# Attention, MLP and expert routing on one core: two chunks keep their low parts in SBUF across a branch, and the branch's verdict is loaded earlier

## The chip, the cores and the metric

The kernel runs on one core of a Trainium2 chip. Engines are written PE (matmuls; PEld is its loading of the stationary operand), DVE, ACT, POOL and SP (which here only issues DMAs). The metric is the device time of one execution in microseconds, median of several runs; lower is better.

## The reference, cut to what matters

```python
x = attention_with_random_features(q, k, v, omega)   # (2304, 512)
h = x @ w_in                                         # 512 -> 2048
m = (h - np.tanh(h)) @ w_out                         # 2048 -> 512
logits = m @ w_gate                                  # 8 experts
# the largest logits are served first; an expert takes at most 288 tokens
for e in range(8):
    out[assigned == e] = np.maximum(m[assigned == e] @ w1[e], 0) @ w2[e]
```

The MLP in the middle is where the change lies.

## The kernel before

**Numbers.** A value in float32 is held as a high part (type fp32r) and a low part (what is left). A product is made of three matmuls: high by high, high by low and low by high. In the code a name with H is a high part, with L a low one.

**Tiling of the MLP.** The 2304 tokens are 6 blocks of 384; the hidden 2048 are 16 chunks `f` of 128. `chunk_ops` makes a chunk of the hidden layer (12 matmuls at L601 to L603 into a PSUM bank, then `h - tanh h` by a polynomial of the range |h| < 0.18: ACT L605 and L625, DVE L626 and L628). `hidden_ops` splits the result into `gH` (ACT, L298) and `gL` (DVE or POOL, L303). `m2_ops` multiplies a chunk by its rows of `w_out`: for each of the block's three token tiles `t` three matmuls at L648 (nine for a chunk), added up over `f` in the PSUM tile `acc[t]`. `wo` is the high part of `w_out` and stays in SBUF; its low parts lie in DRAM (`lows`), and `split_ops` loads that of a chunk into `oL`, a ring of three buffers (SP, L563).

**Blocks 4 and 5.** Their hidden layers are made side by side, chunk by chunk (`mlp_ops`, from "j, lacc4, lprev4" on). The logits of both are summed meanwhile from the hidden layer (`last_logits`, matmuls at L719 and L721, and after the last chunk a copy `lt` on ACT, transposes at L732 and copies to `lg` on DVE at L736 and L737). Block 5 keeps all of `gH5` and `gL5` in SBUF. Block 4 ("the last but one") keeps its 16 high parts in the place of `wi`, which is used up; its low parts go to DRAM (`g4l`, SP L800) through `gLr`, a ring of four buffers, and come back from there (SP L822) when `but_last_ops` multiplies block 4 by `w_out`. Of this, chunks 0 to 2 (`NHERE`) are multiplied before the branch.

**The branch.** `range_ops` works out one number, `over` (DVE, last instruction L868), that says whether some |h| may leave the polynomial's range or some weight is too small. After block 5's logits every engine loads `over` into a register (`values_load`, L1458) and branches on it (L1459). For these inputs the body of the branch, which makes the MLP again in a general way, is skipped.

**Behind the branch**, in order of need: the chunks 3 to 15 of block 4 (117 matmuls), the copies of `acc` to `xm` (`out_ops`), the 16 chunks of block 5 (`last_ops`, 144 matmuls, L648 too), the experts (L1333 to L1354). Beside it runs the routing. `best_ops` finds each token's best expert on DVE (L989 to L993). `search_ops` finds the logit at which the first expert is full, in seven digits: comparisons on DVE (`r_cmp`, L1030), counts on PE (nine matmuls at L1036), the digit on DVE (L1055, L1057) and its spreading by a matmul on PE (L1061), then the next digit. After the digits follow some 10 us of placing, the loads of that expert's weights (`r_wraw`, SP L1249) and the next search.

**What sets the order.** `Plan` is a list scheduler that runs while the program is built. Each operation has engines, a cost, a due time (`plan.at` plus `lag`) and buffers from rings; `Plan.run` gives out the operation that can start first by these costs, and among those of one time the one that is due first. That fixes the order on every engine; on the chip each engine goes through its list and waits by semaphores. `Plan.run` is called once for all before the branch, and once for all behind it, where all engines start at the same planned time. A ring's buffer comes free after the last operation that the plan knows to use it.

Of the kernel before, what the change touches and what calls it, by code (L numbers as in the profile page):

```python
# [185 lines left out]
def tile_kernel(ctx, tc, q, k, v, omega, w_in, w_out, w_gate, w_gate_t, w1, w2, out, dbg=None):  # L186
# [79 lines left out]
    def sring(where, shape, dtype, name, n):  # L266
        return plan.ring(shape, dtype, name, [(where, [f"{name}{i}" for i in range(n)], False)])
# [21 lines left out]
    sr = sring(wmid, [P, BLK], F32, "s", 5)  # L289
    gHr = sring(wmid, [P, BLK], F32R, "gH", 2)  # L290
    gLr = sring(wkeep, [P, BLK], F32R, "gL", 4)
    xmr = sring(wout, [P, DM], F32, "xm", 3)
    g5r = [plan.ring([P, BLK], F32R, n, []) for n in ("gH5", "gL5")]
    mTr = sring(wmid, [P, NC, P], F32, "mT", 1)

    def copy(e, out, in_):
# [7 lines left out]

    bT = Buf(None)

    def omega_ops():
        for i in range(2):  # L310
# [277 lines left out]
    def chunk_ops(j, f, x, wsp, general, gH=None, gL=None):  # L588
# [18 lines left out]
        if general:  # L607

            bg, df = Buf(gen[1]), Buf(gen[1])
            big = lambda: bg.t.bitcast(I32)  # L610
            dif = lambda: df.t
            plan.op(DVE, 0.5, lambda e: V.tensor_scalar(big(), ut(), TMAX ** 2, None, op0=OP.is_gt), r=[u], w=[bg], lag=2.6)
            plan.op(DVE, 0.5, lambda e: V.tensor_scalar(ut(), ut(), TMAX ** 2, None, op0=OP.min), r=[u, bg], w=[u], lag=2.6)
            plan.op(ACT, 0.5, lambda e: nc.scalar.activation(dif(), ph(), AF.Tanh), r=[p], w=[df], lag=2.6)
# [25 lines left out]
    def m2_ops(f, g, wsp, acc, prev, fine=False):  # L640
        gH, gL = g
        oH, oL = wsp
        out = list(prev or [None] * TPB)
        for t in range(TPB):
            def m2(e, i, t=t):
                c = slice(t * P, (t + 1) * P)
                for k in i:
                    nc.tensor.matmul(acc[t].t, (gL if k == 2 else gH).t[:, c], (oL if k == 1 else oH).t,  # L648
                                     start=(f == 0 and k == 0), stop=(f == NF - 1 and k == 2), skip_group_check=True)

            for i in ([0], [1], [2]) if fine else ([0, 1, 2],):
                out[t] = plan.op(PE, 0.235 * len(i), lambda e, i=i, m2=m2: m2(e, i), r=[gH, gL, oH, oL], w=[acc[t]],
                                 after=[out[t]] if out[t] else [], lag=0.65 * t)
        return out

    def out_ops(j, t, acc):
        n = j * TPB + t
        xm = Buf(xmr)
        plan.op({ACT: 0.48, DVE: 0.6}, 0, lambda e: copy(e, xm.t, acc.t), r=[acc], w=[xm])
        return xm, plan.op(SP, 0.47, lambda e: nc.sync.dma_start(ms[n * P + 1:(n + 1) * P + 1, :], xm.t), r=[xm], lag=0.7,  # L660
                           nbytes=P * DM * 4)

    def gate_ops(j, t, xm):
        n = j * TPB + t
        tp, mT, lp = Buf(bank), Buf(mTr), Buf(bank)
        lgb = Buf(None)

        def transposes(e):
            for c in range(NC):
                nc.tensor.transpose(tp.t[:, c * P:(c + 1) * P], xm.t[:, c * P:(c + 1) * P], ident)  # L670
# [73 lines left out]
    def mlp_ops(start, step, general=False):  # L744
# [41 lines left out]
        for f in range(NF):  # L786
            plan.at = start[j] + step[j] * f - LEADI
            wsp = split_ops("wi", f)
            if not general:
# [3 lines left out]
            plan.at += step[j] / 2  # L793
            chunk_ops(j + 1, f, x[j + 1], wsp, general, *g5[f])
            plan.at = start[j] + step[j] * f
            gH, gL = Buf(None, wi[:, f, :BLK]), Buf(gLr)
            gH.readers = list(wbuf["wi", f].readers)
            hidden_ops(s4, gH, gL)
            lprev4 = last_logits(j, lacc4, f, lprev4, gH, gL)
            g4[f] = gH, plan.op(SP, 0.47, lambda e, f=f, gL=gL: nc.sync.dma_start(g4l[f], gL.t.bitcast(F32)), r=[gL],  # L800
                                nbytes=P * BLK * 4, lag=6.8)
            plan.at += step[j] / 2
            lprev = last_logits(j + 1, lacc, f, lprev, *g5[f])

# [3 lines left out]
        for b, old in zip(new, acc4):  # L808
            b.want = old.slot
        acc4[:] = new  # L810
        but_last_ops(0, NHERE, start[j] + step[j] * NF + 1.0, 2.0)

    g4, acc4, prev4 = {}, [], [None]
    NHERE = 3

    def but_last_ops(f0, f1, start, step):

        for f in range(f0, f1):
            plan.at = start + step * f
# [26 lines left out]
    def range_ops():  # L846
# [9 lines left out]
        for i, (z, b) in enumerate(((xn, bxn), (wn, bwn))):  # L856
# [11 lines left out]
        plan.op(DVE, 0.1, lambda e: nc.vector.tensor_tensor(over[:1], mm[:, 0:1], mm[:, 2:3], op=OP.max), r=[bm], w=[bm])  # L868

# [519 lines left out]
    omega_ops()  # L1389
    plan.at = 60.0  # L1390
    zero = Buf(xmr)
    plan.op(POOL, 0.3, lambda e: nc.gpsimd.memset(zero.t[:1], 0.0), w=[zero])
    plan.op(SP, 0.47, lambda e: nc.sync.dma_start(ms[:1, :], zero.t[:1]), r=[zero])
# [202 lines left out]
```

## Time and profile before

| what | us |
|---|---|
| median of 3 runs (918.92, 921.21, 921.49) | 921.21 |
| the profiled execution | 916.65 |
| its span, first to last instruction | 914.7 |
| outside the span (916.65 less 914.7) | 1.95 |
| PE busy within the span | 875.9 (96%) |

A row of the timeline has the start, the duration, the engine and line, what is written and read, and in brackets how long the engine stood before it and what let it go. L numbers are lines of the kernel before. Times within the text are from the start of the span.

### The profile page before, as it was taken

The page shows a single profiled execution, that of the slowest core. Times are in us where ns is not written, and L with a number is a line of the kernel's source. Part 1 is how long each engine was busy: PE and PEld are TensorE (multiplying, and loading weights), DVE is VectorE, ACT ScalarE, POOL GpSimd, SP SyncE. Part 2 cuts the span into 40 slices and gives each one's busy share as a digit, 9 for nine tenths or more (in the row PEclk, how much of TensorE's full clock was granted, in tenths as well). Part 3 has the DMA queues.
Part 4 walks back from the last instruction along what each step waited for, and adds up shares of the span by engine and source line. Part 5 has one row for each costly group of instructions (what it writes and reads, how often), then busy time and mean ns, then how long its engine had stood idle before and what let it go on. Part 6 is the DMA issues. An engine that isn't in the chain of part 4 may idle for free. (4 is left out here: it accounts for less than half of the span.)

```text
span 914.7 us, 17555 instructions
## 1 busy us (share of the span) xinstructions
PE 875.9 (96%) x6168; PEld 770.8 (84%) x6168; DVE 652.2 (71%) x1931; ACT 469.3 (51%) x1015; POOL 253.2 (28%) x271
## 2 busy tenths in 40 slices
PE   8988999999999999999999959899999999999995
PEld 6887888988989888989989937676889888999995
DVE  6899999866588779777778763527687786784520
ACT  5876554545457445655577640203366554465521
POOL 1223433333431345244313230000122322321211
PEclk9999999999999999999999999999999999999998
DMA  8988777876375666434677745845788886877600
GB/s 256 344 283 285 255 248 258 264 246 199 109 241 162 209 207 219 150 105 127 209 289 269 266 164 170 272 127 174 236 266 233 270 226 186 279 186 262 213 28 26
DMA packets 104365, 194.72 MB, mean 213 GB/s; under 512 B 28370, under 2 KB 42834, under 8 KB 104275
## 3 DMA queue, kind: packets, MB, share of 16 engines
q1 hardware_dynamic: 98610, 174.71, 58.0%
q0 software_dynamic: 5664, 18.88, 8.6%
q8 instruction: 49, 0.80, 0.4%
q14 instruction: 42, 0.34, 0.1%
HBM read 150.03 MB, written 34.08 MB: 201 GB/s over the span
## 5 line engine op out<-in xcount | busy, mean ns | idle before, releaser
L648 PE MATMUL acc<-wo,gL 128*128 128x512 f32 x288 | 114.9, 401 | 0.2 <-POOL gL L303 0.2
L601 PE MATMUL bk<-xH,wi 128*128 128x384 f32 x320 | 113.9, 356 | 0.9 <-DVE xt L500 0.9
L602 PE MATMUL bk<-xL,wi 128*128 128x384 f32 x320 | 107.8, 337 | 0.0
L603 PE MATMUL bk<-xH,iL 128*128 128x384 f32 x320 | 107.7, 337 | 0.0
L707 DVE SCALAR_TENSOR_TENSOR lw<-wf,raw 128x512 f32<-128x512 f32 x128 | 103.5, 808 | 2.9 <-POOL wf L704 1.4
L648 PE MATMUL acc<-wo,gH 128*128 128x512 f32 x240 | 101.1, 421 | 0.0
L303 POOL TENSOR_TENSOR gL<-s,gH 128x384 fp32r<-128x384 f32 x52 | 62.7, 1206 | 137.1 <-ACT gH L298 136.0
L648 PE MATMUL acc<-oL,gH 128*128 128x512 f32 x240 | 95.9, 400 | 0.3 <-DVE oL L303 0.3
L438 ACT ACTIVATE phi<-bk,nm 128x128 f32<-128x128 f32 x272 | 77.2, 384 | 34.4 <-DVE nm L441 34.1
L704 POOL TENSOR_TENSOR wf<-oL,wo 128x512 f32<-128x512 f32 x48 | 66.1, 1378 | 68.0 <-DMA oL<-low_wo 63.7
L298 ACT ACTIVATE gH<-s 128x384 fp32r<-128x384 f32 x80 | 42.2, 527 | 63.7 <-DVE s L628 46.3
L626 DVE SCALAR_TENSOR_TENSOR s<-s,bk 128x384 f32<-128x384 f32 x80 | 44.0, 550 | 41.7 <-ACT s L625 40.8
L648 PEld LDWEIGHTS acc<-wo,gL 128*128 128x128 f32 x288 | 54.9, 191 | 13.6 <-POOL gL L303 0.7
L601 PEld LDWEIGHTS bk<-xH,wi 128*128 128x128 f32 x320 | 60.7, 190 | 6.1 <-PE bk L480 1.1
L602 PEld LDWEIGHTS bk<-xL,wi 128*128 128x128 f32 x320 | 60.7, 190 | 2.7
L605 ACT ACTIVATE u<-bk 128x384 f32<-128x384 f32 x80 | 39.2, 491 | 45.2 <-PE bk L603 43.0
L603 PEld LDWEIGHTS bk<-xH,iL 128*128 128x128 f32 x320 | 60.4, 189 | 0.0
L628 DVE SCALAR_TENSOR_TENSOR s<-s,u 128x384 f32<-128x384 f32 x80 | 57.8, 722 | 1.1
L441 DVE TENSOR_REDUCE nm<-bk 128x4 f32<-128x512 f32 (+1 forms) x75 | 46.4, 631 | 12.7 <-PE bk L427 11.1
L648 PEld LDWEIGHTS acc<-wo,gH 128*128 128x128 f32 x240 | 45.7, 190 | 7.0
L648 PEld LDWEIGHTS acc<-oL,gH 128*128 128x128 f32 x240 | 46.0, 191 | 6.4 <-DVE oL L303 0.6
L625 ACT ACTIVATE s<-u,qbias 128x384 f32<-128x384 f32 x80 | 49.3, 616 | 3.8 <-DVE gL L303 1.4
(355 smaller groups left out, 2345.5 us busy)
## 6 DMA issues: line engine op xcount, KB each, us to landing
r_wraw<-in_moe_w_dram SPq DMA_DIRECT2D x48, 512.0 KB, 6.3
iL<-low_wi SPq DMA_DIRECT2D x80, 256.0 KB, 3.2
oL<-low_wo SPq DMA_DIRECT2D x80, 256.0 KB, 2.7
raw<-in_moe_w_in_dram SPq DMA_DIRECT2D x32, 512.0 KB, 5.1
raw<-in_moe_w_out_dram SPq DMA_DIRECT2D x32, 512.0 KB, 4.3
dw<-in_moe_w_dram SPq DMA_DIRECT2D x16, 512.0 KB, 5.9
w1l<-dw SPq DMA_DIRECT2D x16, 512.0 KB, 3.0
s_wraw<-in_moe_w_dram SPq DMA_DIRECT2D x16, 512.0 KB, 5.7
```

Of the source, the lines that this page charges most:

```text
L303: (nc.gpsimd if e == POOL else nc.vector).tensor_tensor(out, in_, high.bitcast(F32), op=OP.subtract)
L438: nc.scalar.activation(ph.t[:, i0 + i, :], pj.t[:, i * M:(i + 1) * M], AF.Exp, bias=nmx.t[:, i0 + i:i0 + i + 1])
L441: plan.op(DVE, 0.1 + 0.125 * n, lambda e, pj=pj, i0=i0, n=n: V.tensor_reduce(nmx.t[:, i0:i0 + n], pj.t[:, :n * M].rearrange("p (i m) -> p ...
L601: nc.tensor.matmul(ph(), piece(iH, c), xH.t[:, c, :], start=(c == 0), stop=False)
L602: nc.tensor.matmul(ph(), piece(iH, c), xL.t[:, c, :], start=False, stop=False)
L603: nc.tensor.matmul(ph(), piece(iL, c), xH.t[:, c, :], start=False, stop=(c == NC - 1))
L625: plan.op(ACT, 0.52, lambda e: nc.scalar.activation(s.t, ut(), AF.Square, bias=qbias), r=[u], w=[s], lag=2.8)
L626: plan.op(DVE, 0.52, lambda e: V.scalar_tensor_tensor(s.t, s.t, QD, ph(), op0=OP.add, op1=OP.mult), r=[p, s], w=[s], lag=3.4)
L628: plan.op(DVE, 0.65, lambda e: V.scalar_tensor_tensor(s.t, s.t, QC, ut(), op0=OP.mult, op1=OP.mult), r=[u, s], w=[s], lag=4.0)
L648: nc.tensor.matmul(acc[t].t, (gL if k == 2 else gH).t[:, c], (oL if k == 1 else oH).t, start=(f == 0 and k == 0), stop=(f == NF - 1 and k ...
L704: plan.op(POOL, 1.45, lambda e: nc.gpsimd.tensor_tensor(w.t, lo.t.bitcast(F32), wo[:, f, :].bitcast(F32), op=OP.add), r=[lo, wbuf["wo", f] ...
L707: x_reads.append(plan.op(DVE, 0.9, lambda e, i=i: nc.vector.scalar_tensor_tensor(scratch.t.bitcast(F32), w.t, 1.0, half(rows[i // 2], i % ...
```

## The change

1. The low parts `gL` of block 4's chunks 14 and 15 (`NKEEP` = 2) go to buffers of their own (`keptr`) and stay there: no store to `g4l`, no load from it, no buffer of `gLr`.
2. The low parts `oL` of `w_out` for these two chunks are loaded during block 4, due 20 us after its start, into two of the three `xm` buffers, and stay there too.
3. Behind the branch `but_last_ops` takes the chunks in the order 14, 15, 3, 4, ..., 13 in place of 3 to 15.
4. `values_load` of `over` becomes an operation of the plan, due 40 us before the planned end of block 4 and not before `over` is written. All engines then have the verdict in a register when they come to the branch.
5. The body of the branch gets one buffer less (`gx` 2 to 1), and two of its writes an order of their own.

```diff
-    xmr = sring(wout, [P, DM], F32, "xm", 3)
+    xmr = sring(wout, [P, DM], F32R, "xm", 3)
+    keptr = plan.ring([P, BLK], F32R, "gLk", [])
...
             plan.at = start[j] + step[j] * f
-            gH, gL = Buf(None, wi[:, f, :BLK]), Buf(gLr)
+            gH, gL = Buf(None, wi[:, f, :BLK]), None if stay else Buf(gLr)
             gH.readers = list(wbuf["wi", f].readers)
+            if stay:
+                gL, oL = kept.setdefault(f, (Buf(keptr), Buf(xmr)))
+                at, plan.at = plan.at, start[j] + 20.0
+                plan.op(SP, 0.47, lambda e, f=f, oL=oL: nc.sync.dma_start(oL.t.bitcast(F32), lows["wo", f]), w=[oL],
+                        after=[stored_low["wo", f]], nbytes=P * DM * 4)
+                plan.at = at
             hidden_ops(s4, gH, gL)
             lprev4 = last_logits(j, lacc4, f, lprev4, gH, gL)
-            g4[f] = gH, plan.op(SP, 0.47, lambda e, f=f, gL=gL: nc.sync.dma_start(g4l[f], gL.t.bitcast(F32)), r=[gL],
-                                nbytes=P * BLK * 4, lag=6.8)
+            g4[f] = gH, None if stay else plan.op(
+                SP, 0.47, lambda e, f=f, gL=gL: nc.sync.dma_start(g4l[f], gL.t.bitcast(F32)), r=[gL],
+                nbytes=P * BLK * 4, lag=6.8)
...
-    def but_last_ops(f0, f1, start, step):
+    def but_last_ops(chunks, start, step):
...
-            gL = Buf(gLr)
-            plan.op(SP, 0.47, lambda e, f=f, gL=gL: nc.sync.dma_start(gL.t.bitcast(F32), g4l[f]), w=[gL], after=[st],
-                    nbytes=P * BLK * 4)
-            prev4[0] = m2_ops(f, (gH, gL), split_ops("wo", f), acc4, prev4[0] if f else [flags[-1]] * TPB)
+            if st:
+                gL = Buf(gLr)
+                plan.op(SP, 0.47, lambda e, f=f, gL=gL: nc.sync.dma_start(gL.t.bitcast(F32), g4l[f]), w=[gL], after=[st],
+                        nbytes=P * BLK * 4)
+                oH, oL = split_ops("wo", f)
+            else:
+                (gL, oL), oH = kept[f], wbuf["wo", f]
+            prev4[0] = m2_ops(f, (gH, gL), (oH, oL), acc4, prev4[0] if f else [flags[-1]] * TPB, end=NF - NKEEP - 1)
...
+        keptr.add(wg5, [f"gLk{i}" for i in range(NKEEP)], t=max(o.end for o in att_ops))
...
+    seen = []
+    plan.at = starts[-1] - 40.0
+    plan.op("-", 0.0, lambda e: seen.append(nc.values_load(over[0:1, 0:1], min_val=0, max_val=1)), r=[bover], early=False)
     plan.run()
     s_pre.close()
-    nover = nc.values_load(over[0:1, 0:1], min_val=0, max_val=1)
-    with tc.If(nover > 0, label="range"), ExitStack() as s_gen:
+    with tc.If(seen[0] > 0, label="range"), ExitStack() as s_gen:
         wgen = pool(s_gen, "wgen", "left")
-        gen[:] = [sring(wgen, [P, H, D], F32, "gx", 2), sring(wgen, [P, BLK], F32, "gd", 3)]
+        gen[:] = [sring(wgen, [P, H, D], F32, "gx", 1), sring(wgen, [P, BLK], F32, "gd", 3)]
...
-    but_last_ops(NHERE, NF, AT_LAST - 1.5 * NF, 1.5)
-    for b in acc4:
+    for b in acc4 + kept_bufs():
         b.left -= 1
+    but_last_ops([*range(NF - NKEEP, NF), *range(NHERE, NF - NKEEP)], AT_LAST - 1.5 * (NF - NHERE), 1.5)
```

The rest of the diff adapts types (`bitcast`) and the flag of the last matmul of a sum (`end`).

## Rows read from the trace of the kernel before

**Rows 1.** The page's first part: busy time of each engine.

```profile
PE 875.9 (96%) x6168; PEld 770.8 (84%) x6168; DVE 652.2 (71%) x1931; ACT 469.3 (51%) x1015; POOL 253.2 (28%) x271
```

**Rows 2.** Windows: stretch, its length, busy time (instructions) by engine, granted clock, DMA.

```profile
core 0: us, PE busy (x) PEld busy (x) DVE busy (x) ACT busy (x) POOL busy (x), PEclk, DMA share, GB/s
...
527.00:542.70 15.70, 11.15 (x52) 6.64 (x50) 10.46 (x19) 8.91 (x18) 5.83 (x5) 1.00 0.45 176
542.70:547.10 4.40, 0.01 (x1) 0.01 (x1) 2.43 (x9) 0.00 (x0) 1.42 (x3) 0.74 0.34 100
547.10:552.20 5.10, 4.54 (x20) 3.33 (x21) 2.22 (x10) 0.00 (x0) 0.00 (x0) 0.55 0.70 234
552.20:576.00 23.80, 23.80 (x143) 16.81 (x142) 8.91 (x47) 0.00 (x0) 0.00 (x0) 1.00 0.57 174
576.00:589.60 13.60, 10.62 (x70) 7.68 (x70) 10.00 (x55) 4.25 (x6) 0.00 (x0) 0.98 0.82 271
...
628.00:640.00 12.00, 10.06 (x70) 8.13 (x69) 11.34 (x43) 7.17 (x13) 1.86 (x2) 1.00 0.81 259
640.00:905.00 265.00, 264.65 (x2189) 241.39 (x2188) 170.61 (x729) 130.05 (x217) 58.58 (x81) 1.00 0.67 206
```

**Rows 3.** Timeline of all engines, end of blocks 4 and 5.

```profile
541.43 0.34 PE L721 MATMUL bk<-gL,vgs 128*8 128x384 f32 x1
...
542.34 0.36 PE L732 MATMUL bk<-ident,lt 16*128 16x16 f32 x3 [0.57 <-ACT lt L298]
...
542.95 0.18 DVE L737 TENSOR_TENSOR lg<-lg,bk 128x24 f32<-128x24 f32 x1
```

**Rows 4.** Timeline of POOL, the last low parts of block 4.

```profile
536.52 1.10 POOL L303 TENSOR_TENSOR gL<-s,wi 128x384 fp32r<-128x384 f32 x1 [2.00 <-DMA g4l<-gL]
539.79 1.02 POOL L303 TENSOR_TENSOR gL<-s,wi 128x384 fp32r<-128x384 f32 x1 [2.17 <-DVE gL L303]
```

**Rows 5.** Line L1458, the loads of the verdict: ns, start.

```profile
L1458 PEldq TENSOR_LOAD <-over x1: 489/489/489, 542.3 to 542.3; - x1
L1458 DVEq TENSOR_LOAD <-over x1: 541/541/541, 543.0 to 543.0; - x1
```

**Rows 6.** Line L1459, the branch: first step behind it on two engines.

```profile
L1459 PEldq EVENT_SEMAPHORE  x1: 51/51/51, 543.4 to 543.4; - x1
...
L1459 DVEq EVENT_SEMAPHORE  x1: 21/21/21, 544.2 to 544.2; - x1
```

**Rows 7.** The chain that ended last, 500 to 600: start, us, what.

```profile
547.09 0.67 PE rp L1036 x9
...
548.48 3.75 PE acc L648 x9
552.24 0.37 PE rp L1036 x9
...
556.60 0.37 PE rp L1036 x9
```

**Rows 8.** Line L822, block 4's low parts loaded from 543.8 on.

```profile
DMA to landing us min/median/max: 2.7/3.9/4.8
```

**Rows 9.** Timelines of DVE and PE around the writing of the verdict.

```profile
483.41 0.14 DVE L868 TENSOR_TENSOR over<-mm 1x1 int32<-1x1 f32 x1
...
483.88 0.33 PE L603 MATMUL acc<-xH,iL 128*128 128x384 f32 x1
484.05 0.33 PE L601 MATMUL acc<-xH,wi 128*128 128x384 f32 x1
```

**Rows 10.** Timeline of PE behind the first chunk of block 5.

```profile
585.33 0.40 PE L648 MATMUL acc<-wo,gL 128*128 128x512 f32 x1
...
588.41 0.52 PE L1036 MATMUL rp<-r_cmp,pairs 128*40 128x62 bf16 x9 [1.98 <-DVE pairs L993]
...
589.60 0.80 PE L648 MATMUL acc<-wo,gH 128*128 128x512 f32 x1
```

**Rows 11.** Line L563, loads of `oL`: issued 560 to 580, then 580.5 to 588.3.

```profile
DMA to landing us min/median/max: 2.6/2.7/2.7
...
DMA to landing us min/median/max: 6.3/8.2/8.9
```

**Rows 12.** The chain that ended last: block 5's matmuls in the second search.

```profile
608.92 5.71 PE acc L648 x24
```

More of the change, by code (lines that the diff above doesn't have):

```diff
@@ L303, in low @@
         (nc.gpsimd if e == POOL else nc.vector).tensor_tensor(out, in_, high.bitcast(F32), op=OP.subtract)
-    bT = Buf(None)
+    bT, bover = Buf(None), Buf(None)
     def omega_ops():
@@ L611, in chunk_ops @@
             dif = lambda: df.t
-            plan.op(DVE, 0.5, lambda e: V.tensor_scalar(big(), ut(), TMAX ** 2, None, op0=OP.is_gt), r=[u], w=[bg], lag=2.6)
+            plan.op(DVE, 0.5, lambda e: V.tensor_scalar(big(), ut(), TMAX ** 2, None, op0=OP.is_gt), r=[u], w=[bg, df], lag=2.6)
             plan.op(DVE, 0.5, lambda e: V.tensor_scalar(ut(), ut(), TMAX ** 2, None, op0=OP.min), r=[u, bg], w=[u], lag=2.6)
-            plan.op(ACT, 0.5, lambda e: nc.scalar.activation(dif(), ph(), AF.Tanh), r=[p], w=[df], lag=2.6)
+            plan.op(ACT, 0.5, lambda e: nc.scalar.activation(dif(), ph(), AF.Tanh), r=[p, bg], w=[df], lag=2.6)
             plan.op(DVE, 0.5, lambda e: V.tensor_tensor(dif(), ph(), dif(), op=OP.subtract), r=[p, df], w=[df], lag=2.6)
@@ L638, in hidden_ops, with m2_ops @@
         plan.op({DVE: 0.55, POOL: 1.15}, 0, lambda e: low(e, gL.t, s.t, gH.t), r=[s, gH], w=[gL], lag=5.8)
-    def m2_ops(f, g, wsp, acc, prev, fine=False):
+    def m2_ops(f, g, wsp, acc, prev, fine=False, end=NF - 1):
         gH, gL = g
@@ L648, in m2 @@
                     nc.tensor.matmul(acc[t].t, (gL if k == 2 else gH).t[:, c], (oL if k == 1 else oH).t,
-                                     start=(f == 0 and k == 0), stop=(f == NF - 1 and k == 2), skip_group_check=True)
+                                     start=(f == 0 and k == 0), stop=(f == end and k == 2), skip_group_check=True)
             for i in ([0], [1], [2]) if fine else ([0, 1, 2],):
@@ L658, in out_ops @@
         xm = Buf(xmr)
-        plan.op({ACT: 0.48, DVE: 0.6}, 0, lambda e: copy(e, xm.t, acc.t), r=[acc], w=[xm])
-        return xm, plan.op(SP, 0.47, lambda e: nc.sync.dma_start(ms[n * P + 1:(n + 1) * P + 1, :], xm.t), r=[xm], lag=0.7,
+        plan.op({ACT: 0.48, DVE: 0.6}, 0, lambda e: copy(e, xm.t.bitcast(F32), acc.t), r=[acc], w=[xm])
+        return xm, plan.op(SP, 0.47, lambda e: nc.sync.dma_start(ms[n * P + 1:(n + 1) * P + 1, :], xm.t.bitcast(F32)), r=[xm], lag=0.7,
                            nbytes=P * DM * 4)
@@ L669, in transposes @@
             for c in range(NC):
-                nc.tensor.transpose(tp.t[:, c * P:(c + 1) * P], xm.t[:, c * P:(c + 1) * P], ident)
+                nc.tensor.transpose(tp.t[:, c * P:(c + 1) * P], xm.t.bitcast(F32)[:, c * P:(c + 1) * P], ident)
         def gate(e):
@@ L795, in mlp_ops @@
             plan.at = start[j] + step[j] * f
-            gH, gL = Buf(None, wi[:, f, :BLK]), Buf(gLr)
+            stay = f >= NF - NKEEP
+            gH, gL = Buf(None, wi[:, f, :BLK]), None if stay else Buf(gLr)
             gH.readers = list(wbuf["wi", f].readers)
+            if stay:
[4 more added lines that the diff above has]
+                plan.at = at
             hidden_ops(s4, gH, gL)
             lprev4 = last_logits(j, lacc4, f, lprev4, gH, gL)
-            g4[f] = gH, plan.op(SP, 0.47, lambda e, f=f, gL=gL: nc.sync.dma_start(g4l[f], gL.t.bitcast(F32)), r=[gL],
-                                nbytes=P * BLK * 4, lag=6.8)
+            g4[f] = gH, None if stay else plan.op(
+                SP, 0.47, lambda e, f=f, gL=gL: nc.sync.dma_start(g4l[f], gL.t.bitcast(F32)), r=[gL],
+                nbytes=P * BLK * 4, lag=6.8)
             plan.at += step[j] / 2
@@ L810, in mlp_ops @@
         acc4[:] = new
-        but_last_ops(0, NHERE, start[j] + step[j] * NF + 1.0, 2.0)
+        for b in kept_bufs() if not general else ():
+            b.left += 1
+        but_last_ops(range(NHERE), start[j] + step[j] * NF + 1.0, 2.0)
     g4, acc4, prev4 = {}, [], [None]
     NHERE = 3
-    def but_last_ops(f0, f1, start, step):
-        for f in range(f0, f1):
-            plan.at = start + step * f
-            gH, st = g4[f]
-            gL = Buf(gLr)
-            plan.op(SP, 0.47, lambda e, f=f, gL=gL: nc.sync.dma_start(gL.t.bitcast(F32), g4l[f]), w=[gL], after=[st],
-                    nbytes=P * BLK * 4)
-            prev4[0] = m2_ops(f, (gH, gL), split_ops("wo", f), acc4, prev4[0] if f else [flags[-1]] * TPB)
+    NKEEP, kept = 2, {}
+    kept_bufs = lambda: [b for f in sorted(kept) for b in kept[f]]
+    def but_last_ops(chunks, start, step):
+        for i, f in enumerate(chunks):
+            plan.at = start + step * i
+            gH, st = g4[f]
+            if st:
[6 more added lines that the diff above has]
+            prev4[0] = m2_ops(f, (gH, gL), (oH, oL), acc4, prev4[0] if f else [flags[-1]] * TPB, end=NF - NKEEP - 1)
     stored, stored4, m5 = [], [], []
@@ L867, in range_ops @@
             mm[:, 0:1], mm[:, 0:1], -1.0, 1.0, op0=OP.mult, op1=OP.add), r=[bm], w=[bm])
-        plan.op(DVE, 0.1, lambda e: nc.vector.tensor_tensor(over[:1], mm[:, 0:1], mm[:, 2:3], op=OP.max), r=[bm], w=[bm])
+        plan.op(DVE, 0.1, lambda e: nc.vector.tensor_tensor(over[:1], mm[:, 0:1], mm[:, 2:3], op=OP.max), r=[bm], w=[bm, bover])
     CAP = NT // E
@@ L1391, in tile_kernel @@
     zero = Buf(xmr)
-    plan.op(POOL, 0.3, lambda e: nc.gpsimd.memset(zero.t[:1], 0.0), w=[zero])
-    plan.op(SP, 0.47, lambda e: nc.sync.dma_start(ms[:1, :], zero.t[:1]), r=[zero])
+    plan.op(POOL, 0.3, lambda e: nc.gpsimd.memset(zero.t[:1].bitcast(F32), 0.0), w=[zero])
+    plan.op(SP, 0.47, lambda e: nc.sync.dma_start(ms[:1, :], zero.t[:1].bitcast(F32)), r=[zero])
     plan.at = 30.0
```

## The prediction

> **What bounds the kernel now.** First the page: PE is busy 96% of the span [rows 1], so time is won only where PE stands or runs slowly, and won time stays won only if PE finds work afterwards. The windows tell where that is [rows 2]. From 640 to 905 PE has 0.35 us of idle time in 265: whatever PE gains before 640 moves the end. Idle or slow stretches near the change are 527 to 542.7 (4.55 us idle), 542.7 to 547.1 (nothing done), 547.1 to 552.2 (granted clock 0.55: mostly the lower of PE's two levels, 1.2 GHz, against 2.4) and 576 to 589.6 (2.98 idle).
>
> The timeline tells what PE waits for. Before the branch the last logits wait for the low part of chunk 15: POOL makes it at 539.79, PE uses it at 541.43, the transposes follow at 542.34 and DVE's last copy at 542.95 [rows 3, 4]. POOL was free from 537.6; its two last low parts stood 2.00 and 2.17 us. The first names a store to `g4l`; the second names a DVE step, but three of the four `gLr` buffers then hold chunks 0 to 2 for PE, so I read both as waits for a buffer. Behind the branch PE is at its first step by 543.4 [rows 6] and has nothing to multiply: the loads of chunk 3 are issued only then and land after 2.7 to 4.8 us [rows 8], and the search's first count, which the plan puts first, starts at 547.09 [rows 7], after DVE, itself past the branch at 544.2 [rows 6], has made the tokens' best logits. Chunk 3 follows after the first digit, at the low clock.
>
> **The change part by part.**
>
> *Low parts of chunks 14 and 15 in own buffers.* Two stores of 196 KB before the branch and two loads behind it go, and chunk 15 no longer waits for a `gLr` buffer. What is late next is the PE: chunk 2's matmuls, held by `acc`, which are in place until about 539.5, then the logits of 13 to 15. At most the POOL wait of 2.17 us falls away, but PE's own queue leaves some 0.4 to 0.8 less on the way to the branch; nothing at worst. I take 0.5.
>
> *Verdict loaded sooner.* At the branch each engine loses one load: 489 ns on PE, 541 on DVE [rows 5]. DVE is on the path (last copy, load, branch, best logits, count), so 0.5. The loads reappear near 483.6, where `over` is written [rows 9]. All five queues carry one; behind it stand PE's chunk matmuls, DVE's and ACT's polynomial steps, SP's loads of `iL` and POOL's splits. From 480 to 527 PE follows itself without a wait (483.88, 484.05, ... [rows 9]), so PE's load counts: between nothing (matmuls already queued cover it) and the 0.49 of its load plus a short wait for `over`; the planned place is just behind the write. I take 0.3. The other loads, about half a us each, are covered by PE's full queue; if that cover failed, one DVE load of 0.54 would show.
>
> By the Trainium skill ("Advanced Engine Details and Errata", Sequencer Loop) an engine's instructions can be queued while the sequencer runs a control instruction, which speaks for nothing on PE; by it the sum would be 0.3 better. The trace agrees as far as it goes: PE's load starts at 542.3, with the transposes of 542.34 still running [rows 3, 5].
>
> *Low parts of `w_out` for 14 and 15.* Two loads of 262 KB move from behind the branch into block 4, on SP ahead of `iL` loads and g4l stores: 0.47 us of planned issue each. They hide under the chunk matmuls. Block 4's other tiles need `xm` only before that and after these chunks; cost nothing, or an `iL` load later by about 0.5 each.
>
> *Chunks 14 and 15 first.* Their 18 matmuls wait for no DMA. In the plan's costs three matmuls are 0.7, and the first count is ready some 2.3 after the branch (five DVE steps of 0.22, pauses of 0.13 and comparisons of 0.76 among them), so 9 or 12 go ahead of the first count, and 6 between it and the matmul of L1061, as in every later digit. One matmul takes 5.71 / 24 = 0.238 [rows 12]. With the verdict and the logits 1.0 sooner, the first count can start at 546.1. PE, free between 542.4 (its own first step less 1.0) and 543.2 (DVE's, should the first matmul wait for that [rows 6]), does 12 matmuls in 2.9, till 545.3 to 546.1. So DVE still sets the count, and PE's pause shrinks from 4.4 to about 1.
>
> Then the first digit. From its count to the next one passes 552.24 - 547.09 = 5.15, in the later digits 556.60 - 552.24 = 4.36 [rows 7]. The nine matmuls within took 3.75 where nine at the high clock take 2.14: the clock costs 1.6. With the clock kept, the digit is a regular one: 0.8 less for the search.
>
> At the second count PE had done 9 of the chunks' matmuls. Now it has done 9 or 12, then 6, then 9: 24 or 27. That is 15 or 18 ahead, 3.6 or 4.3 us; I take 3.9.
>
> Sum: 0.5 + 0.5 + 0.8 + 3.9 - 0.3 = 5.4 us.
>
> *Where it could leak.* PE comes to the end of block 4's 117 matmuls some 5 us sooner, the search only 1.8. Between lies the placing, during which PE in the trace of before ran out at 585.33 and began chunk 1 of block 5 at 589.60 [rows 10]. The loads of `oL` issued there took 6.3 to 8.9 us behind the first expert's weights; those issued before 580 took 2.7 [rows 11]. Issued some 5 us sooner, those of chunks 0 and 1, and perhaps 2, precede the weights (which come 1.8 sooner). Two chunks ready keep a gain of 5.4; with one lost 2.1 go (3.3 left); with all three, PE's pause shrinks, up to 1.2 more (6.6).
>
> The sum against the profiled execution is 916.65 - 5.4 = 911.3. That run lies 4.6 below the median; against the median I predict 921.2 - 5.4 = **915.8**.
>
> **The rivals.**
>
> *B, given back at the weights.* Planned order or DMA put all of block 5's low parts behind the first expert's weights; PE stands until the same `oL` loads as before, which only the search's 1.8 moves, less PE's load: 1.5, so 919.7. For it: PE's stop at 585.33 and the DMA share 0.82 [rows 2, 10]. Against it: the load of chunk 0 was issued before the weights and landed in 2.7 [rows 11].
>
> *C, the clock falls all the same.* The pause of about 1 us falls right behind a stretch where PE was busy 11.15 of 15.7. At the spacing of the nine slow ones (3.75 / 9 = 0.417 in place of 0.238) 12 to 18 matmuls take 2.1 to 3.2 more and delay the count by as much: 2.2 to 3.3 is left, in the middle 918.5. Against it: from 527 to 542.7 the clock stayed 1.00 with 4.55 idle [rows 2]. The Trainium skill ("TensorE: Matmul & The Clock Gate", Part 1) says the array's default is the half clock, and activity releases it; by that rule the fall is a matter of how idle PE looks, and the trace agrees: 0.74, then 0.55, after the pause of 4.4.
>
> *D, slower: the second search is pushed behind block 5.* PE's matmuls of block 5 that are due first go ahead of the second search (24 in a row at 608.92 [rows 12]). If PE no longer lacks `oL`, more digits may be left when block 5 ends, in 628 to 640, where DVE is busy 11.34 of 12 [rows 2] and sets the pace of the first expert. A digit is 8.91 / (23.8 / 4.36) = 1.63 of DVE [rows 2, 7]. It decides from five digits (8.2 against 5.4 + 2.8); all seven give 921.2 - 5.4 + 11.4 = 927.2. Against it: the expert does not need that search, so the plan can put PE's expert matmuls ahead.
>
> *E, it doesn't do what it says.* The plan puts the first count ahead of the kept chunks, or their first matmul waits for the same step of DVE. Then only the two halves before the count (1.0) and the 0.7 from the count's end at 547.76 to the matmuls at 548.48 [rows 7] are won: 919.5.
>
> **How the numbers follow.** Chances: forecast 0.62, B 0.14, C 0.09, D 0.07, E 0.08. About 0.3% (2.8 us) is what a measurement of this kernel can tell. Of C, half is past that bound. Faster: 0.62 + 0.05 = 0.67; same: 0.14 + 0.04 + 0.08 = 0.26; slower: 0.07. The forecast's own range is 914.2 (6.6 and the lower terms at their good ends, 7.0) to 918.5 (2.7: one chunk lost, 0.6 for PE's load, 15 matmuls). For 8 in 10 it reaches to B and E at its upper end, and one us below for runs that spread by 2.6: 912.8 to 920.0.
>
> **What would show it.** Right: no load at the branch; PE matmuls at L648 within 1 us of PE's branch, 24 or 27 before the second count; clock 1.00 between branch and second count; first count 1.0 sooner relative to block 4; from 640 on the same length. Wrong in part: PE waiting for an `oL` behind the weights with one chunk of block 5 done (B); L648 spaced by over 0.4 behind the branch (C); counts at L1036 between the first expert's matmuls (D); a count ahead of the first L648 (E); a gap above 0.6 in PE at the moved load. The prediction is wrong if the new plan moves waits elsewhere, such as before 527, which no row bounds.

## The result, and the profile after

The changed kernel takes 932.27 us (median of 6 runs, 929.67 to 934.2); the kernel before takes 920.07 beside it (6 runs, 918.6 to 923.15). The ratio is 1.0123 with an interval of 1.0097 to 1.0148: slower by about 12 us, where 5.4 us less was forecast. The profiled execution took 934.2, its span is 932.3.

The page's first part says what kind of loss it is: PE is busy for 888.3 us [before: rows 1], with the same 6168 instructions. Of the 17.6 us by which the span is longer, 12.4 are the same work done more slowly and 5.2 are idle time. (The profiled executions lie further apart than the medians: that of the changed kernel is the slowest of its six runs, that of the kernel before is faster than its six.)

```profile
PE 888.3 (95%) x6168; PEld 779.9 (84%) x6168; DVE 655.6 (70%) x1930; ACT 467.7 (50%) x1017; POOL 250.1 (27%) x270
```

The windows of the changed kernel, put where [rows 2] now lie (stretches shifted by what was lost ahead of them) and where PE stands anew:

```profile
core 0: us, PE busy (x) PEld busy (x) DVE busy (x) ACT busy (x) POOL busy (x), PEclk, DMA share, GB/s
460.00:465.00 5.00, 2.27 (x12) 1.93 (x13) 4.05 (x12) 4.23 (x9) 1.00 (x1) 0.78 0.73 268
465.00:470.00 5.00, 5.00 (x20) 4.54 (x18) 2.48 (x3) 1.75 (x5) 1.39 (x1) 0.53 0.40 128
534.00:549.00 15.00, 11.73 (x49) 7.37 (x47) 9.92 (x17) 7.03 (x14) 4.38 (x4) 0.89 0.32 124
549.00:553.60 4.60, 3.41 (x15) 2.44 (x15) 2.61 (x10) 0.00 (x0) 1.42 (x3) 1.00 0.34 103
553.60:558.00 4.40, 4.40 (x26) 3.08 (x25) 2.22 (x10) 0.00 (x0) 0.00 (x0) 1.00 0.82 255
558.00:582.00 24.00, 24.00 (x142) 16.97 (x142) 8.91 (x47) 0.00 (x0) 0.00 (x0) 1.00 0.50 158
595.00:606.00 11.00, 8.61 (x31) 5.76 (x31) 2.22 (x10) 3.94 (x4) 0.28 (x1) 0.70 0.53 194
662.00:682.00 20.00, 16.66 (x106) 13.49 (x105) 8.12 (x46) 5.67 (x9) 2.71 (x4) 0.74 0.63 184
```

Behind the branch (549.0 to 582) the change does what it was forecast to: in the stretch where PE had done nothing it is busy 3.41 of 4.60, and the granted clock stays at 1.00 where it was 0.74 and 0.55 [rows 2]. The losses lie elsewhere, in three places, each idle time followed by a stretch near the lower level: 460 to 470 (0.78, 0.53), 595 to 606 (0.70), 662 to 682 (0.74). The 0.89 of 534 to 549 is no fourth: e1_late_loads below has the same clock ahead of the branch (0.89 from 526 to 541) and passes the branch sooner than the kernel before.

**The branch.** The chain that ended last, of the changed kernel, from the branch on [before: rows 7]:

```profile
549.59 2.56 PE acc L649 x10
552.15 0.96 issue
553.11 0.63 PE acc L649 x2
553.73 0.37 PE rp L1055 x9
554.10 1.58 PE acc L649 x6
555.69 0.11 PE rp L1080
555.79 2.30 PE acc L649 x9
558.09 0.25 PE rp L1055 x5
558.34 0.89 PE acc L649 x3
559.24 0.22 PE rp L1055 x4
...
563.45 0.37 PE rp L1055 x9
```

12 matmuls stand ahead of the first count, then 6, then 9: 27 before the second count, where the kernel before had 9. A count is nine matmuls, and here the plan has parted the second one: its first five stand behind 27 matmuls of `w_out`, its last four behind 30. So it is complete 3 matmuls late, and the search gains nothing: from the first count to the third pass 9.72 us (553.73 to 563.45), 9.51 in the kernel before (547.09 to 556.60 [rows 7]), where two regular digits take 8.72. Not forecast, too, is the 0.96 us in which PE stands and the profile shows nothing that it waits for.

**Block 3's end.** The kept low parts of `w_out` go into two of the three `xm` buffers. Line L803, their loads (start of the first and last), of the changed kernel:

```profile
L803 SPq DMA_DIRECT2D xm<-low_wo x2: 327/350/373, 154.1 to 168.7; - x2
```

They run at 154 and 169, some 300 us ahead of the place at which the code sets them (20 us into block 4): the due time settles only which of the ready steps goes first, and these were ready. (A step of this plan starts no sooner than its due time only where it is given `early=False`, as the load of the verdict is.) From then on every output tile passes through one `xm` buffer. PE's timeline at the end of block 3 shows what that does:

```profile
460.98 0.34 PE L722 MATMUL kv<-gL,vgs 128*8 128x384 f32 x1 [1.02 <-DVE mm L885]
461.47 1.06 PE L675 MATMUL bk<-wg,mT 128*128 128x8 f32 x8
464.12 0.69 PE L602 MATMUL acc<-xH,wi 128*128 128x384 f32 x1 [1.60 <-ACT xm L299]
```

**Block 5.** The chain of the changed kernel, 596 to 626 [before: rows 12]:

```profile
593.14 6.77 DMA r_xg<-ms,r_ix
...
599.95 2.44 PE bd L1324 x8
602.39 8.14 PE acc L649 x27
610.53 0.25 PE rp L1055 x5
610.79 7.73 PE acc L649 x33
618.51 0.23 PE rp L1055 x4
```

Two things. The first transposes of expert 0's gathered rows (L1324) stand further ahead in PE's order, and PE waits 1.79 us for the rows (timeline of the changed kernel):

```profile
599.95 1.98 PE L1324 MATMUL bd<-ident,r_xg 128*128 128x128 f32 x6 [1.79 <-DMA r_xg<-ms,r_ix]
```

And the two halves of one count of the second search (x5, x4) have 27 and 33 matmuls of block 5 in front of them: this is the pushing that rival D spoke of. The ranks that follow from the second search come at 640.8 in the changed kernel; in the kernel before they came at 629.0:

```profile
640.83 0.19 PE L1144 MATMUL rp<-r_M,onesb 128*128 128x36 bf16 x1 [1.05 <-DVE r_M L1133]
```

```profile
629.02 0.19 PE L1125 MATMUL rp<-r_M,onesb 128*128 128x36 bf16 x1
```

**Expert 0 and 1.** POOL's timeline of the changed kernel, and of the kernel before:

```profile
659.72 1.18 POOL L1308 DMA_INDIRECT r_xg<-ms,r_ig  x1 [6.95 <-DVE r_cmp L1049]
661.20 1.00 POOL L1308 DMA_INDIRECT r_xg<-ms,r_ig  x1 [0.30 <-DVE r_base L1069]
662.18 1.03 POOL L1287 DMA_DIRECT2D s_ewL<-r_wraw  x1
```

```profile
653.65 1.06 POOL L1289 DMA_INDIRECT r_xg<-ms,r_ig  x1 [13.72 <-DVE r_pre L1043]
654.68 0.97 POOL L1268 DMA_DIRECT2D s_ewL<-r_wraw  x1
```

Expert 1's gathers need the second search. In the changed kernel two of them, the first after standing 6.95 us, are ahead of the accumulating DMA that finishes expert 0's low weights, issued at 662.18. In the kernel before one is ahead of it, and it was issued at 654.68. PE, in expert 0's second product, waits for that DMA (chain that ended last and timeline of the changed kernel), and runs slowly afterwards:

```profile
662.18 10.03 DMA s_ewL<-r_wraw
```

```profile
672.26 0.61 PE L1373 MATMUL bd<-s_hH,s_ewL 128*128 128x288 f32 x1 [3.34 <-DMA s_ewL<-r_wraw]
```

**Positions.** The table, worked out from the traces, follows one execution of each kernel through the program. A number is the start of an instruction in that kernel less its start in the kernel before, less the same difference at one fixed place, the 505th matmul of the second product (block 3, 414.61 us in the kernel before). That place is subtracted because the executions shown differ by up to 5.8 us there already. "s1 count" and "s1 last" are the first and the last of the seven counts of the first search, "s2 last" the last count of the second, "blk 5 start" the first matmul of block 5 by `w_out`, "E0" and "E1" expert 0 and 1, "y end" the last of E0's second product.

```
                    branch   s1     s1     blk 5    s2     E0     E0      E1     end of
                    (DVE)  count   last    start   last   start  y end   start   span
changed kernel       +3.5   +4.0   +4.3    -0.7    +9.2   +2.3   +10.4   +11.5   +15.1
e2_verdict_alone      0.0    0.0   -0.1    -0.1    -0.2   -0.2    -0.1    -0.1    -0.1
e1_late_loads        -0.4   +0.7   +1.0    -4.1    +5.0   -2.0    +8.1    +9.3   +10.3
e5_gather_behind     +3.4   +3.4   +3.7    -1.3    +8.7   +2.0    +0.6    +9.1   +10.1
e4_old_order         -0.2   -0.2   +0.2    +0.2    +4.8   +2.5    +5.7    +5.1    +6.8
e8_search_due        +3.2   +3.2   +3.5    -1.6    -7.9   +1.6    +4.1    +3.8    +5.5
e7_both              -0.4   +0.3   +0.6    -4.4   -12.9   -3.4    -1.2    -1.8    -0.5
e9_both_gather       -0.5    0.0   +0.2    -4.8   -13.7   -4.2    -4.7    +3.8    +2.3
e11_before_due       +0.2   +0.2   +1.4    +1.4   -13.2   +2.5    +3.9    +3.3    +4.4
e12_due3             -0.3   +0.4   +0.7    -4.4    -1.1   +1.1    +4.5    +4.0    +7.2
e13_old_order_due3   -0.5   -0.6   +0.9    +0.9    -2.5   +1.4    +2.0    +1.4    +3.1
e14_due3_turn        -0.4   +0.3   +0.6    -4.4    -4.5   -3.7    -1.9    -2.5    +0.3
e15_three            -0.2   +0.6   +0.9    -4.1   -13.9   -3.6    -2.2    -2.7    -1.4
e16_late_turn        -0.4   +0.4   +0.7    -4.4    +3.3   -3.6    +5.1    +6.2    +8.4
```

A row is one execution, and the runs of one kernel spread by 3 to 14 us, so the table says where a difference arises, and the medians how large it is. In every row the end lies 0.2 to 2.9 us above the difference of the medians: the profiled execution of the kernel before was a fast one. Rows are better compared with each other than with zero.

### The profile page after: what moved, and what is told of

Its sections match the earlier page's. It is cut to its first block, busy times and chain, and to the rows that moved or that the text cites. A ratio compares the mean times of both kernels' runs of the same rounds, so it can differ in the third digit from the quotient of the medians.

```text
span 932.3 us, 17537 instructions
## 1 busy us (share of the span) xinstructions
PE 888.3 (95%) x6168; PEld 779.9 (84%) x6168; DVE 655.6 (70%) x1930; ACT 467.7 (50%) x1017; POOL 250.1 (27%) x270
## 5 line engine op out<-in xcount | busy, mean ns | idle before, releaser
L602 PE MATMUL bk<-xH,wi 128*128 128x384 f32 x320 | 114.1, 357 | 1.0 <-DVE xt L501 1.0
L649 PE MATMUL acc<-wo,gL 128*128 128x512 f32 x282 | 112.8, 400 | 0.0
L304 POOL TENSOR_TENSOR gL<-s,gH 128x384 fp32r<-128x384 f32 x52 | 60.8, 1169 | 144.1 <-ACT gH L299 135.5
L602 PEld LDWEIGHTS bk<-xH,wi 128*128 128x128 f32 x320 | 60.7, 190 | 7.1 <-PE bk L481 1.2
```

The lines of the kernel that those rows point to most:

```text
L304: (nc.gpsimd if e == POOL else nc.vector).tensor_tensor(out, in_, high.bitcast(F32), op=OP.subtract)
L602: nc.tensor.matmul(ph(), piece(iH, c), xH.t[:, c, :], start=(c == 0), stop=False)
```

## The experiments

Theory at the start: (a) the early loads starve `xm` and cost some 4.7 us by block 4; (b) the pushed second search, through the place of expert 1's gathers in POOL's queue, costs some 8 us; (c) the early transposes cost some 3. Rivals: the early loads of the verdict cost (a); the late second search costs (b) by itself, whatever POOL's order; the new order of chunks costs as such. Each experiment is the changed kernel with the edit shown, unless it says otherwise.

**e1_late_loads.** The loads wait for block 3's tiles to have been read.

```diff
-                        after=[stored_low["wo", f]], nbytes=P * DM * 4)
+                        after=[stored_low["wo", f]] + [o for b in used.values() for o in b.readers], nbytes=P * DM * 4)
```

> The changed kernel with one edit: the two kept low parts of w_out are loaded only after block 3's output tiles have gone through the xm buffers (they were loaded some 300 us before their use and held two of the three xm buffers). Theory: the waits for xm and for the gate at the end of block 3 (1.60 and 1.02 us) and the 1.2 GHz stretch of 6.8 us from 462.8 go; the position at block 4's start returns by about 4.7 us and carries to the end, some 927.5 us (926 to 929). Rival (the early loads of the verdict at 462 cost the time there): the clock still falls at 462.8 and the time stays within 1.5 us of the changed kernel's 932.

Measured 927.92 (ratio to the kernel before 1.0097, 1.0064 to 1.013). The loads now start at 460.0; the window at block 3's end keeps its clock:

```profile
460.00:470.00 10.00, 9.04 (x58) 8.37 (x59) 8.41 (x15) 7.02 (x15) 1.96 (x2) 1.00 0.93 316
```

(a) holds: 4.4 us by the medians, 4.8 in the table, 2.4 by the two ratios to the kernel before, which was run anew beside each. All of the rest is still lost behind expert 0's start, where this kernel arrives 2.0 us ahead of the kernel before.

**e2_verdict_alone.** The kernel before, with `values_load` moved into the plan as in the change, and nothing else.

> The kernel before with the early load of the verdict alone; chunk order and buffers as before. Theory: the loads cost nothing where they stand and the branch follows the last block sooner by about 1 us: 919 us (917.5 to 920.5). Rival (the loads on all engines in the middle of block 4 delay its start and bring the lower clock): 923 or more.

Measured 918.22 (0.9984, 0.9961 to 1.0008). The early loads cost nothing, which ends that rival, and gain nothing that shows at the first count (0.0 in the table). At the branch itself they do gain: from the last copy of the logits to its first step behind the branch DVE stands 1.65 us in the kernel before and 1.03 here.

```profile
544.78 0.30 DVE L989 TENSOR_REDUCE r_m<-lg 128x18 f32<-128x144 f32 x1 [1.65 <-DVEq L1459]
```

```profile
543.73 0.30 DVE L989 TENSOR_REDUCE r_m<-lg 128x18 f32<-128x144 f32 x1 [1.03 <-DVEq L1461]
```

The 0.6 won there is lost ahead of it in this execution: its granted clock was 0.51 from 533.2 to 536.7, where the kernel before had 1.00 [rows 2], and its last copy of the logits comes 0.6 later by the table's measure.

**e5_gather_behind.** Expert 1's gathers behind expert 0's last accumulating DMA.

```diff
-                r=[ix], w=[t], after=stored if p else stored4, late=5.0)
+                r=[ix], w=[t], after=stored + ([acc_dma[0]] if p == 1 else []) if p else stored4, late=5.0)
```

> The changed kernel with one edit: on POOL's queue, the gathers of expert 1's rows stand behind the last accumulating DMA of expert 0's low weights instead of two of them ahead of it. Theory: the wait of 3.34 us of expert 0's second product for its low weights and most of the 1.2 GHz stretch of 10.2 us from 671.1 go, some 8 us: 924 us (922 to 927). Rival (the second search, 12 us later than before, sets expert 1's start by itself): expert 0 ends 8 us sooner, expert 1 waits for its rows that much longer, and the time stays within 2 us of 932.

Measured 927.98 (1.0087, 1.0056 to 1.0117): half of what the theory asked for, and more than the rival's 2 us. In the table expert 0's loss is gone (+0.6 at its end, +10.4 in the changed kernel), and expert 1 starts at +9.1, 2.4 sooner than in the changed kernel. Most of the wait has only moved, as the rival had it. PE's timeline of this run between the two experts:

```profile
672.44 0.30 PE L1373 MATMUL bd<-s_hH,s_ewL 128*128 128x288 f32 x1
672.77 0.19 PE L1144 MATMUL rp<-r_M,onesb 128*128 128x36 bf16 x1
...
679.77 0.18 PE L1080 MATMUL rp<-id,r_d 8*128 8x8 bf16 x1 [1.56 <-DVE r_cond L1076]
680.78 0.65 PE L1212 MATMUL rp<-r_ohh,r_lid 128*32 128x18 bf16 x18 [0.83 <-DVE r_pre L1086]
681.36 0.61 PE L1352 MATMUL be<-s_xgH,s_ewH 128*128 128x288 f32 x1
```

So the theory's (b) falls in its place: not POOL's queue, the late search. The theory from here on: the plan prefers block 5's chunks (due at -42.7 and after) to the second search (due at -31) whenever both are ready. With the chunks ready sooner, the search is late, and expert 1 waits for it in one way or another ("s2 last" in the table: +9.2 in the changed kernel, +8.7 here, +5.0 in e1_late_loads).

**e4_old_order.** e1_late_loads, with the chunks behind the branch as 3 to 15.

> The edit of the late loads, and the chunks of block 4 behind the branch in their old order (3 to 15, the kept ones last). POOL's queue still has expert 1's gathers ahead of expert 0's last accumulating DMA. Theory: the forecast gain behind the branch (4.9 us) is given up, the wait of expert 0's second product stays: 928 to 932. Rival (the new order of the chunks, by pushing the second search back, is what costs the time at expert 0): 922 or less.

Measured 926.55 (1.0065, 1.0042 to 1.0089), below the theory's range and far from the rival's. The new order is not what costs most: with the old one 1.4 us are saved by the medians, 3.5 in the table, and the rest stays. The second search is late here too (45 matmuls of `w_out` ahead of one count, +4.8 at its last).

**e8_search_due** and **e7_both.** The second search due 15 us sooner, in the changed kernel and in e1_late_loads.

```diff
-        plan.at = PHASE * p - RLEAD[p > 0]
+        plan.at = PHASE * p - RLEAD[p > 0] - (15.0 if p == 1 else 0.0)
```

> The changed kernel with one edit: the second search is due 15 us sooner in the plan, ahead of block 5's chunks; in the plan its first three counts then stand 9, 7 and 13 matmuls of w_out apart (changed kernel: 36, 45 and 12; kernel before: 9, 18 and 60). POOL still has expert 1's gathers ahead of the accumulating DMAs of expert 0. Theory (the late second search is what costs the time at experts 0 and 1): expert 1's first product follows expert 0's last within 2 us, and the time is that of the changed kernel less some 8 to 10 us of its 12.8 gained between expert 0's start and expert 4's: 923 (921 to 926), the loss ahead of block 4's end staying. Rival (the place of the gathers in POOL's queue costs it): expert 0's second product waits for its low weights as before, 928 or more.

> The changed kernel with two edits: the late loads of the kept low parts of w_out, and the second search due 15 us sooner. Theory: both losses gone, and the forecast gain behind the branch is what stays: expert 0 starts some 2.7 us sooner than in the kernel before, as in the run with the late loads alone, and the end with it: 917 (914.5 to 919). Rival (the gathers' place in POOL's queue): 922 or more. Rival (another search or DMA sets the end once these are away): 919 to 923.

Measured 921.64 (1.0019, 0.9996 to 1.0042) and 917.88 (0.9989, 0.9965 to 1.0012). The edit takes 10.6 us off the changed kernel and 10.0 off e1_late_loads by the medians (9.6 and 9.9 by the ratios), and POOL still has the gathers ahead of two accumulating DMAs: the revised theory holds. The difference of the two, run side by side, is 3.8 us by the medians, 2.8 by the ratios: (a) a second time.

**e9_both_gather.** e7_both with the edit of e5_gather_behind.

> As the run with both edits, and expert 1's gathers behind expert 0's last accumulating DMA on POOL. Theory: within 1.5 us of the run with both edits, since with an early search the gathers' input is there when their turn comes and nothing queues behind them. Rival (the gathers' place): 4 us or more below it.

Measured 920.27 (1.0018, 0.9999 to 1.0038), 2.4 above e7_both where 1.5 was allowed. In the table expert 1 starts 8.5 us after expert 0's lead of 4.7 would let it: with the gathers later, their transposes and the third search's counts fall between the experts. So with an early search the gathers' place costs nothing, and moving them costs a little.

**e11_before_due.** The kernel before with the search due 15 us sooner.

> The kernel before with the second search due 15 us sooner, nothing else. Theory: expert 1 already followed expert 0 within 1 us there, so there is nothing to gain: within 2 us of the kernel before, 920. Rival (an early second search is a gain of its own, whatever the change does): 916 or less.

Measured 922.68 (1.003, 1.0014 to 1.0046): a small loss, somewhat more than the 2 us that was allowed. The edit is no gain of its own, so what it gives the changed kernel is what the change had taken.

**e12_due3, e13_old_order_due3, e14_due3_turn.** Late loads with the search due 3 us sooner; the same with the old order of chunks; the same with the new order and the gathers of expert 0 planned to land 4 us later (`late=9.0`), which puts the first transposes behind 16 more matmuls.

> Late loads of the kept low parts, and the second search due 3 us sooner instead of 15: its third count then stands 223 matmuls of w_out behind the start of the stretch, near the 237 of the kernel before (the run with both edits: 186), and two accumulating DMAs of expert 0 stand ahead of expert 1's gathers on POOL as in the kernel before (the run with both edits: one). Theory: the second search due 15 us sooner brings the third search in among expert 0's products as well and costs there what the kernel before with that edit lost (0.3%, 2.7 us); with 3 us this goes, and the time is 1 to 3 us under the run with both edits: 915.5 (913.5 to 917.5). Rival (a search that ends later than in the kernel before delays expert 1 however little): 918 to 923.

> The same two edits, and the chunks behind the branch in their old order, the kept ones last. Theory: what the order of the chunks is worth by itself is the difference to the run with the two edits alone; by the positions of the second product in the runs with late loads, some 3 us of the 5.4 forecast: 918.5 (917 to 920.5). Rival (keeping the low parts in SBUF is what gains, in whatever order): the same time as with the new order within 1 us.

> Late loads, the second search due 3 us sooner, and the first transposes of expert 0's gathered rows later in TensorE's order: 16 matmuls behind their place in the changed kernel. Theory: the wait of 1.79 us for the rows and the 1.2 GHz stretch of 6.8 us behind it, some 3 us in the changed kernel, go: 2 to 3 us under the run with the two edits alone, 913 (911 to 915.5). Rival (the rows come in time wherever the start of block 5 is early): no difference within 1 us.

Measured 925.35 (1.0046, 1.0022 to 1.0071), 920.94 (0.9998, 0.9977 to 1.002) and 918.92 (0.9992, 0.9974 to 1.001). All three lie above their ranges, the first by 8 us, the others by 0.4 and 3.4. The window of the first, and that of e14_due3_turn, at the start of block 5:

```profile
581.00:600.00 19.00, 15.92 (x80) 11.01 (x80) 9.73 (x45) 5.29 (x5) 2.99 (x3) 0.76 0.79 291
```

```profile
581.00:600.00 19.00, 16.14 (x89) 11.71 (x87) 9.87 (x46) 5.54 (x6) 2.98 (x3) 0.91 0.85 304
```

PE is busy equally long; the clock, 0.76 against 0.91, leaves the second with 9 instructions more done. By the medians the later transposes are worth 6.4 us, in the table 4.8 at expert 0's start and 6.9 at the end: (c), larger than thought. Its mechanism is not the wait for the rows that the theory named: in e12_due3 PE waits for them 0.21 us only, and what differs is the clock. Why the clock is low there was not tried:

```profile
595.14 2.44 PE L1325 MATMUL bd<-ident,r_xg 128*128 128x128 f32 x8 [0.21 <-DMA r_xg<-ms,r_ix]
```

The old order comes out between the two, so with the search due 3 us sooner the order of the chunks decides nothing that can be told.

**e15_three, e16_late_turn.** Late loads and later transposes, with the search due 15 us sooner, and with the search left alone.

> Late loads, the second search due 15 us sooner, and the first transposes of expert 0's rows 14 matmuls later. Theory: the position at block 5's second chunk, +0.6 with the two edits alone, gains the 2 to 3 us that the later transposes gave with the search due 3 us sooner, and about half of it reaches the end, as there: 916 (913.5 to 918.5). Rival (with an early search its counts already cover the wait for the rows): within 1 us of the run with the two edits, 918.

> Late loads and the later first transposes, the second search left where the changed kernel has it (36 and 45 matmuls of w_out between its first counts). Theory (the second search sets when expert 1 starts): expert 0 starts 2 to 3 us sooner than with the late loads alone, expert 1 does not, and the time is that of the late loads alone within 1.5 us, 927.5 (926 to 929). Rival (the three losses simply add): 924.5 to 925.5.

(The +0.6 in the first of these texts is no position in the table's sense: it was read 6 matmuls late, and the 2.5 us by which that execution of e7_both was behind at the fixed place were not taken off. At the fifth chunk of block 5 e7_both is 3.4 us ahead.) Measured 916.45 (0.9977, 0.9957 to 0.9997) and 927.63 (1.01, 1.0078 to 1.0121). With the late search the later transposes are worth 0.3 us by the medians, 1.9 in the table: by the time, the losses do not add, as the theory had it. The table fits it only in part: expert 1 starts 3.1 us sooner than in e1_late_loads, which the theory excluded, but the second search ends 1.7 sooner too. With all three undone the kernel has the lowest median of the study, 0.23% below the kernel before, with an interval that just excludes no difference; one such among thirteen kernels proves little, and e7_both (0.9989) and e2_verdict_alone (0.9984) cannot be told from it.

## Why the prediction was wrong, step by step

- *Own buffers for the low parts of 14 and 15* (0.5) and *verdict loaded sooner* (0.5, less 0.3 on PE): DVE passes the branch 0.4 sooner in e1_late_loads and 0.2 to 0.5 in the other runs with late loads and the new order, against a forecast of 0.7 net. The load's share is as forecast at the branch itself (1.65 to 1.03 us on DVE); that the verdict alone gives 0.0 in the table lies ahead of the branch, where the clocks of the two executions differ. What the buffers of their own give was not measured alone. Right in sign, about half in size. PE's load does fit under its queue nearly whole: in e1_late_loads PE stands 0.36 us at that place.
- *Chunks 14 and 15 first*: 27 matmuls before the first half of the second count and 30 before its second half, and from then on 21 ahead of the kernel before (45 against 24 at the third count; at 0.238 each 5.0 us, against 3.9 taken). The clock stays at 1.00, but the 0.8 for a regular digit is not won, as the second count is parted. Wrong, too, was "DVE still sets the count": the 12 matmuls take 3.2 us (2.56 + 0.63 in the chain above), and PE's stop among them, 0.96 there and 1.45 in e1_late_loads, makes PE set it. In e1_late_loads the first count is 0.7 later where 1.0 sooner was forecast. So PE is further ahead with its matmuls than forecast and the search further behind: at its last count the first search is 1.0 later in e1_late_loads and 0.6 in e7_both, where 1.8 sooner was forecast, and block 5 starts 4.1 and 4.4 sooner. Of the sum's 5.4 these 4.1 to 4.4 are there at the end of block 4: this part is sound, up to its terms for the search.
- *Low parts of `w_out` for 14 and 15*: **the first step that failed**. "Block 4's other tiles need `xm` only before that and after these chunks; cost nothing" took the due time in the code for the start. The loads start 300 us sooner and hold two of three buffers through blocks 1 to 3. Measured: 4.4 (e1_late_loads) and 3.8 (e8 against e7) by the medians, 2.4 and 2.8 by the ratios. The prediction's last sentence on what would show it, waits "before 527, which no row bounds", named the gap but gave it no price.
- *Where it could leak* and *rival D*: **the second step that failed, and the larger**. The leak was priced for `oL` alone, 2.1 per chunk lost. D named the right cause, the second search pushed back by block 5's matmuls, but gave it a chance of 0.07, on the ground that "the expert does not need that search, so the plan can put PE's expert matmuls ahead". It did put them ahead: expert 0 starts only 2.3 late. Then expert 0 waited for weights queued behind gathers that need that search, and expert 1 for its own rows: these two users of the search are what the prediction left out, and with them 9.6 to 10.8 us in the table (search due, without and with late loads). That D's price, 11.4, is near this is luck, and so is that 927.2 and the 4.4 of the early loads make 931.6 (932.27 was measured). D had seven digits left when block 5 ends, each at DVE's pace; in the changed kernel one of the seven counts is left then (at 636.5, with block 5's last matmul at 634.0).
- *Rival B* (given back at the weights): in e1_late_loads block 5 starts 4.1 ahead and expert 0 2.0. Half of the gain is given back in between, but no wait of PE there names `oL`. With the first transposes of the gathered rows later (e16_late_turn) 3.6 of 4.4 are kept, so it is mostly their place that costs.
- *Rival C* (the clock falls behind the branch): not so, 1.00 from 549 to 582. The Trainium skill ("TensorE: Matmul & The Clock Gate", Part 1) has activity release the full clock, and the trace agrees here, with PE busy 3.41 of 4.60; and at the other places, where idle time of 2.7 us is followed by a stretch at 0.53 and the stretch with 2.4 idle is at 0.70. At the first place the position lost 4.7 us (a matmul of L602 in block 4 started at 475.77, at 468.49 in the kernel before, less the 2.5 lost earlier) to waits of 2.6: with the clock, they cost nearly twice their length. At the second it lost 3.0 (table, from block 5's start to expert 0's) around a wait of 1.8, but e16_late_turn loses 0.8 without that wait.
- *Rival E* (does not do what it says): not so, by the chain behind the branch.

Not undone by any run: what of the 3.6 us that e15_three leads by at expert 0's start is lost among the experts (1.4 are left at the end). From expert 0's start to expert 1's (633.4 to 670.3) its PE stands 2.48 us, in the kernel before 0.40 (636.3 to 672.3). Its two waits are for the digits of the third search, which now stands among expert 0's products:

```profile
635.58 0.18 PE L1081 MATMUL rp<-id,r_d 8*128 8x8 bf16 x1 [1.77 <-DVE r_cond L1077]
643.67 0.17 PE L1081 MATMUL rp<-id,r_d 8*128 8x8 bf16 x1 [0.71 <-DVE r_cond L1077]
```

## What to carry to other kernels

Where a planner orders the work, a due time is not a start: a step moved or added may run as soon as its inputs and a buffer are there, and what it holds from then on has to be counted from that moment. And a gain ahead of a planned stretch is a new input to the plan: ask which ready work will now outrank the work that the next stage waits for, and price the next user of that work, not only the next in line. When a wait is cured and the time stays, follow the position past the cure: in e5_gather_behind the loss moved from expert 0 to expert 1 and so pointed to its true source, which e8_search_due and e7_both then showed.

## What the runs showed of the hardware

- In all ten kernels with the new order PE stops once, 8 or 10 matmuls behind the branch, for 0.43 (e8_search_due) to 1.45 us (e1_late_loads) with nothing shown that it waits for; 0.96 in the changed kernel. The Trainium skill ("Runtime: NRT & Kernel Launch", Instruction fetch mechanics) says that a taken branch breaks the sequential prefetch of instructions and can stall the engine; no run here tells whether that is the cause.
- Five loads of one word at once took 729 to 826 ns at 462 us in the changed kernel, 470 to 546 ns at 482.6 in e2_verdict_alone. The cause was not tried.
- Executions differ early: e11_before_due, which has the operations of the kernel before up to the branch, is 5.4 us behind it at 414 us already and 7.2 at the first matmul by `w_out` (88.5 us in the kernel before), more than most of the effects studied here. The cause was not tried. Positions counted from a fixed place show where an edit acts in spite of this.
